# A long convolution and a bilinear layer on one core: the first layer's Strassen scheme laid over the pair of weights, in chunks of 768 tokens

## The chip, the core and the metric

The kernel runs on one core of one Trainium2 chip. A core has engines that run side by side and meet at semaphores: TensorE (PE) multiplies matrices and writes PSUM; VectorE (DVE) and ScalarE (ACT) work on SBUF and PSUM; GpSimd (POOL) works on SBUF; SyncE (SP) issues DMA transfers, which ACT's queue does too. PSUM has eight banks; one holds 512 float32 columns in each of 128 partitions. The metric is the device time of one execution in microseconds, the median of the runs.

## The reference

All is float32. For each of 8 sequences of 3072 tokens with 256 channels:

```python
X = np.fft.rfft(x, axis=1)
y = np.fft.irfft(X * (filt_r + 1j * filt_i), n=3072, axis=1)   # 256 channels
a = y @ w_a          # 256 x 1536
b = y @ w_b          # 256 x 1536
out = (a * b) @ w_out   # 1536 x 256
```

## The kernel before

Accuracy near float32 comes from splitting: each operand of a fast matmul is a rounded high part and the low rest, and a product takes three passes (high by high, high by low, low by high).

**The transforms.** A sequence is written as 128 x 24 tokens. Per sequence (a batch; the text counts them from 0 to 7) there are 12 first steps (`split_x`, `s1`, `store_z`: two rows of 24 each, through DRAM `z`), 16 second steps (`s2`: the short transform and the product with the filter on DVE; `split_y`; `is1`: the inverse short transform, into DRAM `td`), and the inverse long step `is2`, which makes the tokens of one chunk out of `tt` (loaded from `td`). The sequence has 6 chunks of 512 tokens. `is2` also makes the seven combinations of Strassen's scheme, as `ah` (high) and `al` (low): two of the four quarters come from one half of the channels, two from the other.

**The two layers.** For each chunk there are 6 visits, one for each pair `p` of 128-column blocks of the weights. In a visit each of `w_a` and `w_b` is multiplied by Strassen's scheme (the variant with seven products and shared sums): the quarters are two halves of the channels, two halves of the tokens (256 each), two blocks of the pair. A product (`product`) writes the a and the b part side by side into one bank of 512 columns, 2 x 3 matmuls of 256 columns; numbers 1, 6, 7 and 4 go to bank x, 2 to y, 5 and 3 to z. ACT copies the partial results out (lines 932, 940, 942, 968) and DVE adds the rest (937, 957, 959). `parts` multiplies a by b (line 678), `split` makes `gh` on ACT and `gl` on POOL (686, 687), and `project` adds the second layer's products into banks po0 and po1: 12 matmuls of 512 columns a visit. Every product and projection matmul is issued in `mm` (line 226), with a weight load of its own. PSUM: x has two buffers, y, z, po0, po1, f0 and f1 (transforms) one each.

**The order.** It is written out by hand. Each visit has slots 2v and 2v + 1; `plan` and `early` hold the transform steps of the next sequence and the `is2` of the next chunk. Steps of odd slots run in the next visit after product 6, steps of even slots before product 4. A visit projects one half of the visit before (`f0`) and the other half of the one before that (`f1`).

**The first sequence.** Its transforms run ahead of the first visit (the front, 91 us), with plain float32 matmuls. The weights arrive as float64 and are converted on DVE, ACT and POOL (`conv_...`: fields, power, sign, high, low, value, combine, halves); 11 of the 18 pieces before the first visit, seven beside visits (`BESIDE`, `stream_weights`). So that late weights aren't needed early, sequence 0 takes chunks 0 and 1 half by half, and `keep` holds half a sum in the buffers of the filter (line 706), which `store` adds later.

Of the kernel before, what the change touches and what calls it, by code (L numbers as in the profile page):

```python
# [19 lines left out]
N1, N2 = 128, 24  # L20
# [4 lines left out]
NC = 6  # L25
# [4 lines left out]
BESIDE = {i: (11 + i, None) for i in range(7)}  # L30
# [55 lines left out]
def _tables():  # L86
# [100 lines left out]
    gc = g.reshape(NC, 4, 128, N1).transpose(0, 2, 1, 3)  # L187
# [31 lines left out]
def fft_filter_bilinear_kernel(ctx: ExitStack, tc, x, x0, filt, fny, filt0, fny0, wa, wb, wo, s1c, gc, fc, fl, ic, sc, s1f, ff, fi, out):  # L219
# [13 lines left out]
    p2 = pool("p2", 2)  # L233
# [20 lines left out]
    ps_x, ps_h, ps_o, ps_f = pool("ps_x", 2, PSUM), pool("ps_h", 1, PSUM), pool("ps_o", 1, PSUM), pool("ps_f", 1, PSUM)  # L254
# [11 lines left out]
    def give_weights(p, where):  # L266
        wab[p] = [[where.tile([128, 7, 128], F32R, name=f"w{m}{h}{p}") for h in "hl"] for m in "ab"]
# [23 lines left out]
    def conv_fields(w):  # L291
        if streaming:
            sc = bank_f([128, 512], I32, streaming[-1])
        else:
            sc = ps_x.tile([128, 512], I32, name="sc", tag="x")
# [29 lines left out]
    spare, pair = [], {}  # L325
# [119 lines left out]

    def s2(b, i):
        zt, fr, fm = held.pop(("z", b, i)), filts[i % 2][:, 0], filts[i % 2][:, 1]
        ps = bank_f([128, 2, D])
        turn(i, fct, flt, zt[0], zt[1], ps)
        y = later[0].tile([128, 2, D], F32, name="y", tag="e1")  # L450
# [9 lines left out]
        nc.vector.tensor_tensor(out=y, in0=y, in1=v, op=ALU.add)  # L460
# [18 lines left out]
    def first_const(n0, n1):  # L479
        if "sf" not in held:  # L480
            held["sf"] = p2.tile([128, 13, 128], F32, name="sf", tag="ah")
            held["sh"] = p2.tile([128, NI, 128], F32R, name="sh", tag="ah"), p2.tile([128, NI, 128], F32R, name="sl", tag="al")
        nc.sync.dma_start(out=held["sf"][:, n0:n1], in_=s1f[:, n0:n1])

    def first_split(i0, i1):
        (sh, sl), sf = held["sh"], held["sf"][:, i0 + 1:i1 + 1]
        nc.scalar.copy(out=sh[:, i0:i1], in_=sf)
        nc.vector.tensor_tensor(out=sl[:, i0:i1], in0=sf, in1=f32(sh[:, i0:i1]), op=ALU.subtract)
# [71 lines left out]
    def first_swap(i):  # L560
# [3 lines left out]
        if not swapped:  # L564
            swapped["w"] = p2.tile([128, 3, 2, D], F32, name="fs", tag="al")
# [38 lines left out]
    def first_t():  # L604
        tt = p2.tile([128, 4, D], F32, name="tt", tag="tt", bufs=1)
        gt = p2.tile([128, 4, N1], F32, name="gt", tag="gt", bufs=1)
        nc.sync.dma_start(out=gt, in_=gc[0])
        ah = p2.tile([128, 7, 256], F32R, name="ah", tag="ah")
        al = p2.tile([128, 7, 256], F32R, name="al", tag="al")
        held["t", 0, 0] = tt, gt, ah, al  # L610

    def load_td(tt, b, c, i, queues):

        for j, queue in enumerate(queues):
            to = tt[8 * i.start:8 * i.stop].rearrange("(p j) n d -> j p n d", j=2)[j]
            queue.dma_start(out=to, in_=td[b][i, :, 4 * c:4 * c + 4, j].rearrange("i q n d -> (i q) n d"))
# [405 lines left out]
```

## Time and profile before

| | us |
|---|---|
| median of 3 runs | 2464.78 (2461.64 to 2466.12) |
| the profiled execution | 2464.96 |
| its span, first to last instruction | 2463.2 |
| first visit starts | 91.07 |
| second sequence's visits start | 411.53 |
| sequence 3's visits start and end | 1001.85, 1297.02 |
| last sequence's visits start | 2182.52 |

The page of the profile gives each engine's busy time, the chain of work that ended last, groups of instructions with mean lengths and the idle time before them, and DMA issues. The starts of visits were read from the timeline of PE. A matmul's row is longer than the time until the next one starts, because matmuls overlap; what one costs is the distance between two starts.

### The profile page before, as it was taken

To read this page: it belongs to the slowest core of one execution; us is meant where nothing else is said; L and a number is where in the kernel's file an instruction comes from. 1 tells how busy PE (TensorE), PEld (TensorE's weight loads), DVE (VectorE), ACT (ScalarE), POOL (GpSimd) and SP (SyncE) were. 2 spreads that over 40 slices of the span, in tenths; PEclk is the share of its full clock that TensorE was granted. 3 is DMA by queue.
4 is the path that set the end of the run, shared out by engine and by line. 5 is a ranking of instruction groups with operands and counts; after the bars stand their busy time and mean duration, and the time that the engine had idled before them with its cause. 6 is when DMAs were issued, how large, how long until landed. Compare 5 with 4: busy or idle time off the path is not lost.

```text
span 2463.2 us, 46508 instructions
## 1 busy us (share of the span) xinstructions
PE 2420.0 (98%) x17478; PEld 2263.9 (92%) x17478; DVE 1780.7 (72%) x2511; ACT 1405.0 (57%) x2480; POOL 1223.0 (50%) x926
## 2 busy tenths in 40 slices
PE   7889999999999999999999999999999999999999
PEld 3588999999999999999999999999999999999998
DVE  6775996569955798568976589656996569955554
ACT  5755555555556555565555555565555655555454
POOL 4765454545545554454545545454454545534333
PEclk9999999999999999999999999999999999999999
DMA  9437442544334443245523454145432444310100
GB/s 303 160 127 239 148 134 71 171 143 142 116 102 142 152 154 114 88 146 160 159 80 112 157 158 139 63 145 166 142 121 78 161 144 149 108 39 22 44 22 18
DMA packets 209397, 310.21 MB, mean 126 GB/s; under 512 B 19186, under 2 KB 119476, under 8 KB 209092
## 3 DMA queue, kind: packets, MB, share of 16 engines
q1 hardware_dynamic: 166580, 230.55, 30.3%
q10 hardware_dynamic: 42592, 76.70, 8.9%
q8 instruction: 137, 2.24, 0.4%
q14 instruction: 88, 0.72, 0.1%
HBM read 202.31 MB, written 108.45 MB: 126 GB/s over the span
## 4 chain that ended last, share of the span: by engine, by line
PE 93%; DMA 2%; issue 2%; ACT 1%; DVE 1%; POOL 1%; SPq 0%; ACTq 0%; POOLq 0%; DVEq 0%
PE x L226 30%; PE po L226 30%; PE z L226 15%; PE y L226 7%; PE ps L635 3%; PE ps L226 3%; PE ps L441 2%; PE ps L442 2%; DMA filt<-in_filt 1%; PE ps L556 0%; POOL xl L393 0%; PE ps L524 0%; DMA zf<-z 0%; DVE g L678 0%; DMA gt<-in_gc 0%
## 5 line engine op out<-in xcount | busy, mean ns | idle before, releaser
L687 POOL TENSOR_TENSOR gl<-g,gh 128x512 fp32r<-128x512 f32 x574 | 745.1, 1301 | 788.8 <-ACT gh L686 762.5
L678 DVE TENSOR_TENSOR g<-c 128x512 f32<-128x512 f32 x576 | 509.1, 884 | 271.1 <-ACT c L968 134.0
L968 ACT COPY c<-x 128x512 f32<-128x512 f32 x288 | 169.2, 587 | 688.0 <-PE x L226 685.1
L686 ACT CAST gh<-g 128x512 fp32r<-128x512 f32 x576 | 357.1, 620 | 52.8 <-PE po L226 26.7
L226 PE MATMUL po<-gh,woh 128*128 128x512 f32 x1152 | 369.5, 388 | 2.6 <-DVE filt L706 2.6
L226 PE MATMUL po<-gl,woh 128*128 128x512 f32 x1152 | 359.8, 380 | 0.0
L226 PE MATMUL po<-gh,wol 128*128 128x512 f32 x1152 | 359.8, 380 | 0.0
L226 PE MATMUL x<-ah,wah 128*128 128x256 f32 x1152 | 316.8, 275 | 7.0 <-ACT c L932 4.5
L226 PE MATMUL x<-al,wah 128*128 128x256 f32 x1152 | 317.1, 275 | 0.1
L226 PE MATMUL x<-ah,wal 128*128 128x256 f32 x1152 | 316.9, 275 | 0.0
L226 PE MATMUL x<-ah,wbh 128*128 128x256 f32 x1152 | 316.9, 275 | 0.0
L226 PE MATMUL x<-al,wbh 128*128 128x256 f32 x1152 | 316.9, 275 | 0.0
L226 PE MATMUL x<-ah,wbl 128*128 128x256 f32 x1152 | 316.9, 275 | 0.0
L957 DVE TENSOR_TENSOR c<-x,c 128x512 f32<-128x512 f32 x288 | 197.9, 687 | 155.3 <-PE x L226 149.9
L226 PEld LDWEIGHTS po<-gl,woh 128*128 128x128 f32 x1152 | 217.3, 189 | 32.6 <-DVE gl L687 0.4
L226 PEld LDWEIGHTS po<-gh,wol 128*128 128x128 f32 x1152 | 218.3, 190 | 29.3
L226 PEld LDWEIGHTS x<-ah,wah 128*128 128x128 f32 x1152 | 219.5, 191 | 26.0 <-ACT c L932 5.9
L226 PEld LDWEIGHTS x<-al,wah 128*128 128x128 f32 x1152 | 219.6, 191 | 15.3 <-DVE al L646 0.3
L656 POOL TENSOR_TENSOR al<-t,ah 128x512 fp32r<-128x512 f32 x96 | 146.3, 1544 | 152.3 <-ACT ah L655 152.3
L226 PEld LDWEIGHTS x<-ah,wal 128*128 128x128 f32 x1152 | 221.3, 192 | 0.0
L226 PEld LDWEIGHTS x<-ah,wbh 128*128 128x128 f32 x1152 | 221.3, 192 | 0.0
L226 PEld LDWEIGHTS x<-al,wbh 128*128 128x128 f32 x1152 | 221.3, 192 | 0.0
(145 smaller groups left out, 6067.4 us busy)
## 6 DMA issues: line engine op xcount, KB each, us to landing
z<-zh ACTq DMA_DIRECT2D x112, 256.0 KB, 2.5
filt<-in_filt SPq DMA_DIRECT2D x112, 256.0 KB, 2.6
zth<-z SPq DMA_DIRECT2D x112, 256.0 KB, 3.0
tt<-td SPq DMA_DIRECT2D x94, 256.0 KB, 3.9
out<-ot SPq DMA_DIRECT2D x47, 512.0 KB, 3.0
td<-t ACTq DMA_DIRECT2D x114, 192.0 KB, 2.1
xt<-in_x SPq DMA_DIRECT2D x84, 256.0 KB, 4.2
st<-s1d SPq DMA_DIRECT2D x84, 256.0 KB, 2.7
```

What stands on the lines that cost most here:

```text
L226: nc.tensor.matmul(out, w, m, **kw)
L441: nc.tensor.matmul(out, w[:, 0], hi, start=True, stop=False)
L442: nc.tensor.matmul(out, wl[:, 0], lo, start=False, stop=True)
L635: nc.tensor.matmul(to, tt[:, n, 128 * k:128 * k + 128], gt[:, n].rearrange("p (k a) -> p k a", k=2), start=True, stop=True)
L656: nc.gpsimd.tensor_tensor(out=al[:, 3 + i:5 + i], in0=t[:, i:i + 2], in1=f32(ah[:, 3 + i:5 + i]), op=ALU.subtract)
L678: nc.vector.tensor_tensor(out=gt, in0=g[:, :, 0], in1=g[:, :, 1], op=ALU.mult)
L686: nc.scalar.copy(out=gh, in_=gt)
L687: low.tensor_tensor(out=gl, in0=gt, in1=f32(gh), op=ALU.subtract)
L957: nc.vector.tensor_tensor(out=c1[:, 1], in0=bx, in1=c1[:, 1], op=ALU.add)
L968: nc.scalar.copy(out=c1[:, 0], in_=bx)
```

## The change

Strassen's scheme is laid over the pair (w_a, w_b): its two column blocks are now the same 128 columns of `w_a` and of `w_b`, where they were two blocks of one matrix. One unit `u` of 12 is a visit; a product has three matmuls, and its result is one half of the tokens of a chunk. A chunk has 768 tokens, so there are 4 a sequence, 48 visits a sequence for 36, and a product's matmul has 384 columns. The projection of a visit has 768 columns: 512 in po0 or po1 and 256 in po2, which both output halves share. x and y have one bank each and swap roles from visit to visit.

Moved: the add of `y` and `v` to POOL (`add_y`), and the filter's DVE work to the end of the visit (`late`); low halves of `al` from POOL to DVE; the stores of z from ACT's queue to SP's; part of the output copies from DVE to ACT; both halves of a visit are projected two visits later; `ah` and `al` lie in alternating pools. The slots of the transform steps are new: second steps stand four slots apart in most sequences, `is2` comes in four pieces, and first steps begin before the end of the round before. Sequence 0 takes its chunks in plain order, and `keep` is gone.

```diff
-NC = 6
+NC = 4
+NM = N2 // NC
+TH = NM // 2 * N1
+FULL = 512
-BESIDE = {i: (11 + i, None) for i in range(7)}
+BESIDE = {v: (11 + i, None) for i, v in enumerate((0, 1, 2, 4, 5, 6, 7))}
...
-    ps_x, ps_h, ps_o, ps_f = pool("ps_x", 2, PSUM), pool("ps_h", 1, PSUM), pool("ps_o", 1, PSUM), pool("ps_f", 1, PSUM)
+    ps_h, ps_o, ps_f = pool("ps_h", 1, PSUM), pool("ps_o", 1, PSUM), pool("ps_f", 1, PSUM)
...
     def conv_value(w):
-        v = f32(t) if k == 2 else pair[p][:, k, 0:4].rearrange("p a n -> p (a n)")
-        nc.gpsimd.tensor_tensor(out=v, in0=f32(t), in1=f32(s), op=ALU.mult)
+        if k == 2:
+            nc.gpsimd.tensor_tensor(out=t, in0=t, in1=s, op=ALU.mult)
+        else:
+            for i in range(2):
+                nc.gpsimd.tensor_tensor(
...
     def store_z(b, i):
-        nc.scalar.dma_start(out=zd[b][0][:, 2 * i:2 * i + 2], in_=f32(zh))
+        nc.sync.dma_start(out=zd[b][0][:, 2 * i:2 * i + 2], in_=f32(zh))
...
-        nc.vector.tensor_tensor(out=y, in0=y, in1=v, op=ALU.add)
+    def add_y(b, i):
+        y, v = held["y", b, i]
+        nc.gpsimd.tensor_tensor(out=y, in0=y, in1=v, op=ALU.add)
...
     def is2(b, c, k):
+        if k > 1:
+            i = 2 * k - 4
             nc.scalar.copy(out=ah[:, 3 + i:5 + i], in_=t[:, i:i + 2])
-            nc.gpsimd.tensor_tensor(out=al[:, 3 + i:5 + i], in0=t[:, i:i + 2], in1=f32(ah[:, 3 + i:5 + i]), op=ALU.subtract)
+            v.tensor_tensor(out=al[:, 3 + i:5 + i], in0=t[:, i:i + 2], in1=f32(ah[:, 3 + i:5 + i]), op=ALU.subtract)
+            return
...
-    def product(b, c, p, i, bank, first=False):
+    def product(b, c, u, i, bank, first=False):
         m, n = FACTORS[i]
-        for k in range(2):
-            wh, wl = wab[p][k]
-            for q, (w, v) in enumerate(((wh, ah), (wh, al), (wl, ah))):
-                mm(
-                    bank[:, k], w[:, m], v[:, n], start=first and k == 0 and q == 0, stop=q == 2, skip_group_check=True
-                )
+        ah, al = held["t", b, c][2:]
+        wh, wl = wab[u // 2][u % 2]
+        for q, (w, v) in enumerate(((wh, ah), (wh, al), (wl, ah))):
+            mm(bank, w[:, m], v[:, n], start=first and q == 0, stop=q == 2, skip_group_check=True)
...
+    def project(r, i):
+        passes = [(k, q, *w) for q, w in enumerate(((wo_h, gh), (wo_l, gh), (wo_h, gl))) for k in range(2)]
+        if begins or ends:
+            passes.sort(key=lambda e: e[0] if begins else -e[0])
+        for k, q, w, g in passes:
+            to, g = (po[2][:, i], g[:, FULL:]) if k else (po[i], g[:, :FULL])
...
+    def store(r, i):
+        if i:
+            nc.vector.tensor_copy(out=ot[:, :, FULL:], in_=po[2])
+        nc.scalar.copy(out=ot[:, i, :FULL], in_=po[i])
...
+                bx, bz = bank("xy"[v % 2]), bank("z")
+                product(b, c, u, 1, bx, True)
+                nc.scalar.copy(out=c00, in_=bx)
+                if prev:
+                    split(prev[-1], 0)
+                product(b, c, u, 5, bz, True)
+                nc.scalar.copy(out=c10, in_=bz)
+                by = bank("yx"[v % 2])
+                product(b, c, u, 2, by, True)
+                convert(1)
+                product(b, c, u, 6, bx)
+                nc.scalar.copy(out=c01, in_=bx)
+                if prev:
+                    split(prev[-1], 1)
+                convert(3)
+                for what, at_slot in after:
+                    run(what, at_slot)
+                run(early, slot)
+                if one:
+                    project(one, 0)
...
+                product(b, c, u, 7, bx)
+                nc.vector.tensor_tensor(out=c10, in0=bx, in1=c10, op=ALU.add)
+                nc.vector.tensor_tensor(out=c00, in0=by, in1=c00, op=ALU.add)
+                product(b, c, u, 3, bz)
+                nc.vector.tensor_tensor(out=c01, in0=bz, in1=c01, op=ALU.add)
+                nc.vector.tensor_tensor(out=c01, in0=c01, in1=c10, op=ALU.mult)
+                convert(5)
+                run(plan, slot)
+                if one:
+                    project(one, 1)
...
+                product(b, c, u, 4, bx)
+                nc.scalar.copy(out=c11, in_=bx)
+                nc.vector.tensor_tensor(out=c00, in0=c00, in1=c11, op=ALU.mult)
+                r["gated"] = c01, c00
+                for fn, *args in late:
+                    fn(*args)
```

## Rows read from the trace of the kernel before

**Rows 1.** The page, parts 1 (busy time by engine) and 4 (chain that ended last)

```profile
PE 2420.0 (98%) x17478; PEld 2263.9 (92%) x17478; DVE 1780.7 (72%) x2511; ACT 1405.0 (57%) x2480; POOL 1223.0 (50%) x926
...
PE 93%; DMA 2%; issue 2%; ACT 1%; DVE 1%; POOL 1%; SPq 0%; ACTq 0%; POOLq 0%; DVEq 0%
```

**Rows 2.** Windows: length, each engine's busy us (instructions), PE clock, DMA; three stretches

```profile
91.07:411.53 320.46, 301.98 (x2165) 282.48 (x2166) 249.11 (x351) 187.68 (x333) 178.56 (x130) 0.99 0.45 145
91.07:165.10 74.03, 62.73 (x430) 56.69 (x431) 62.90 (x94) 47.99 (x83) 54.56 (x36) 0.98 0.29 102
1001.85:1297.02 295.17, 295.17 (x2185) 281.14 (x2183) 219.52 (x305) 170.50 (x302) 148.25 (x113) 1.00 0.42 131
```

**Rows 3.** Timeline of PE, one visit of batch 7: start us, us, instruction

```profile
2182.52 0.28 PE L226 MATMUL x<-ah,wah 128*128 128x256 f32 x1
...
2186.49 0.27 PE L226 MATMUL x<-ah,wah 128*128 128x256 f32 x1
...
2187.83 0.60 PE L226 MATMUL po<-gh,woh 128*128 128x512 f32 x2
...
2189.80 0.28 PE L226 MATMUL x<-ah,wah 128*128 128x256 f32 x1
```

**Rows 4.** The page, part 5: weight loads (PEld) | busy, mean ns | idle before

```profile
L226 PEld LDWEIGHTS po<-gh,wol 128*128 128x128 f32 x1152 | 218.3, 190 | 29.3
...
L226 PEld LDWEIGHTS x<-ah,wal 128*128 128x128 f32 x1152 | 221.3, 192 | 0.0
```

**Rows 5.** Groups of instructions by shape, batch 3: ACT, DVE, POOL

```profile
L686 ACT CAST gh<-g 128x512 fp32r<-128x512 f32 x72 | 44.7, 621 | 5.8 <-DVE g L678 3.3 <-PE po L226 2.4
...
L968 ACT COPY c<-x 128x512 f32<-128x512 f32 x36 | 21.1, 587 | 87.6 <-PE x L226 87.6
...
L957 DVE TENSOR_TENSOR c<-x,c 128x512 f32<-128x512 f32 x36 | 24.7, 687 | 16.5 <-PE x L226 15.8
...
L687 POOL TENSOR_TENSOR gl<-g,gh 128x512 fp32r<-128x512 f32 x72 | 93.6, 1303 | 93.8 <-ACT gh L686 92.5 <-PE x L226 1.3
```

**Rows 6.** Groups by shape, ACT, the last 23 us

```profile
L725 ACT COPY ol<-po 128x256 f32<-128x256 f32 x1 | 0.4, 372 | 2.3 <-PE po L226 2.3
```

**Rows 7.** Timeline of all engines from 95.6 to 96.9 us

```profile
95.67 0.49 DVE L299 TENSOR_SCALAR t<-raw 128x512 int32<-128x512 int32 x1
...
95.83 0.28 PE L226 MATMUL x<-ah,wbl 128*128 128x256 f32 x1
96.14 0.58 ACT L942 COPY c<-x 128x512 f32<-128x512 f32 x1
...
96.78 0.19 PEld L226 LDWEIGHTS x<-ah,wah 128*128 128x128 f32 x1 [0.86 <-ACT c L942]
```

**Rows 8.** Waits of PE in batch 0: us in total, times, longest us

```profile
PE x L226 <- ACT c L932: 4.5, 6, 1.4
...
PE po L226 <- DVE filt L706: 2.6, 2, 1.9
```

**Rows 9.** Groups by shape, POOL and DVE, 91 to 165 us

```profile
L687 POOL TENSOR_TENSOR gl<-g,gh 128x512 fp32r<-128x512 f32 x14 | 19.0, 1354 | 13.7 <-ACT gh L686 13.7
...
L656 POOL TENSOR_TENSOR al<-t,ah 128x512 fp32r<-128x512 f32 x4 | 5.5, 1388 | 2.6 <-ACT ah L655 2.6
...
L299 DVE TENSOR_SCALAR t<-raw 128x512 int32<-128x512 int32 x7 | 8.9, 1269 | 0.0
...
L339 DVE TENSOR_TENSOR m<-m 128x256 f32<-128x256 f32 x12 | 4.5, 419 | 0.1
```

**Rows 10.** Timeline of all engines from 78 to 99 us

```profile
77.83 2.11 POOL L339 TENSOR_TENSOR m<-m 128x256 f32<-128x256 f32 x3
...
88.83 2.02 PE L635 MATMUL ps<-gt,tt 128*128 128x128 f32 x16 [1.86 <-DMA tt<-td]
```

**Rows 11.** Timeline of all engines from 2450 us on

```profile
2452.56 0.69 DVE L678 TENSOR_TENSOR g<-c 128x512 f32<-128x512 f32 x1
```

**Rows 12.** The page, part 6: DMA issues, KB each, median us to landing

```profile
tt<-td SPq DMA_DIRECT2D x94, 256.0 KB, 3.9
```

More of the change, by code (lines that the diff above doesn't have):

```diff
@@ L266, in give_weights @@
     def give_weights(p, where):
-        wab[p] = [[where.tile([128, 7, 128], F32R, name=f"w{m}{h}{p}") for h in "hl"] for m in "ab"]
+        wab[p] = [[where.tile([128, 7, 128], F32R, name=f"w{m}{h}{p}") for h in "hl"] for m in "ef"]
     for p in range(NP - LATE):
@@ new lines, in is2 @@
+            held["t", b, c] += [where.tile([128, 7, TH], F32R, name=n, tag=n, bufs=1) for n in ("ah", "al")]
+            ah, al = held["t", b, c][2:]
+            t = held["b", b, c] = moe[0].tile([128, 4, TH], F32, name="t", tag="ot")
+            ps = is2_half(b, c, 0, 0)
+            nc.scalar.copy(out=t[:, 1], in_=ps)
+            ps = is2_half(b, c, 0, 1)
+            nc.scalar.copy(out=ah[:, 0], in_=t[:, 1])
+            v.tensor_tensor(out=t[:, 0], in0=ps, in1=t[:, 1], op=ALU.subtract)
@@ new lines, in product, with piece, split @@
+        wh, wl = wab[u // 2][u % 2]
+        for q, (w, v) in enumerate(((wh, ah), (wh, al), (wl, ah))):
+            mm(bank, w[:, m], v[:, n], start=first and q == 0, stop=q == 2, skip_group_check=True)
+    def bank(name):
+        return ps_h.tile([128, TH], F32, name=name, tag=name)
+    def piece(name, bufs=1):
+        return moe[0].tile([128, TH], F32, name=name, tag=name, bufs=bufs)
+    def split(r, h, low=nc.gpsimd):
+        if "g" not in r:
+            r["g"] = [moe[0].tile([128, 2, TH], F32R, name=n, tag=n, bufs=2) for n in ("gh", "gl")]
+        (gh, gl), gt = r["g"], r["gated"][h]
+        nc.scalar.copy(out=gh[:, h], in_=gt)
+        low.tensor_tensor(out=gl[:, h], in0=gt, in1=f32(gh[:, h]), op=ALU.subtract)
@@ L856, in fft_filter_bilinear_kernel @@
         steps(POST)
-        is2(0, 0, 0)
-        is2(0, 0, 1)
+        for k in range(4):
+            is2(0, 0, k)
         steps(LAST)
@@ new lines, in fft_filter_bilinear_kernel, with at, run @@
+        FORMED = (
[3 rows of a table added]
+        )
+        ROUND = 2 * NC * NF
+        plan, early = {}, {}
+        def at(slot, fn, *args, when=plan):
+            when.setdefault(slot, []).append((fn, *args))
+        def run(what, slot):
+            for fn, *args in what.pop(slot, ()):
+                fn(*args)
+        at(7, nc.sync.dma_start, s1d, s1c)
+        for t, v, d in ((fct, fc, fcd), (flt, fl, fld), (ict, ic, icd)):
+            at(8, nc.sync.dma_start, d, v)
+            at(10, nc.sync.dma_start, f32(t), d)
@@ L919, in run @@
-            def run(what, slot):
-                for fn, *args in what.get(slot, ()):
-                    fn(*args)
-            for v, (c, p) in enumerate(VISITS if b == 0 else [(c, p) for c in range(NC) for p in range(NP)]):
-                slot = 2 * v
-                halves = b == 0 and c < 2
-                convert = (lambda site: stream_weights(v, site)) if b == 0 else (lambda site: None)
-                r = {"at": (b, c, p), "from": NP // 2 if halves and p >= NP // 2 else 0, "to": NP // 2 - 1 if halves and p < NP // 2 else NP - 1}
-                bx, by, bz = bank("x"), bank("y"), bank("z")
-                c0 = moe[0].tile([128, 2, 2, 256], F32, name="c0", tag="c0")
-                c1 = r["c1"] = moe[0].tile([128, 2, 2, 256], F32, name="c1", tag="c1", bufs=2)
-                product(b, c, p, 1, bx, True)
-                nc.scalar.copy(out=c0[:, 0], in_=bx)
-                product(b, c, p, 2, by, True)
-                if prev:
-                    split(prev[-1], "f0")
-                    parts(prev[-1], prev[-1]["c1"], "f1")
-                nc.vector.tensor_tensor(out=c0[:, 0], in0=by, in1=c0[:, 0], op=ALU.add)
+                        at(t, load_z, n, i + 3)
```

305 lines of the change are left out of this document (136 added, 169 removed), and 3 rows, old and new, of the table FORMED.

## The prediction

> **What bounds the kernel now.** I read the page first: TensorE (PE) is busy 98% of the span and the chain that ended last is 93% PE [rows 1]. Busy time alone proves little, since matmuls are pipelined, so I cut the span into batches. Batch 3 shows PE busy for 295.17 of 295.17 us while VectorE (DVE) has 219.5, ScalarE (ACT) 170.5 and GpSimd (POOL) 148.3 us of work [rows 2]; the view of waits names none of PE's between 411 and 2453 us. So from batch 1 on the time is what PE needs to issue its matmuls. Batch 0 takes 320.46 us [rows 2], 25.3 more, in waits. The front takes 91 us. The profiled execution took 2464.96 us, 1.76 more than its span and 0.2 from the median of the runs; I sum against it.
>
> What a matmul costs is read from start to start, not from its row's length. In a visit without transform steps, twelve matmuls of 256 columns start between 2186.49 and 2187.83 us: 111.7 ns each. The whole visit, 42 of these and 12 of 512 columns, takes 7.28 us, so one of 512 takes (7280 - 42 x 111.7) / 12 = 215.8 ns [rows 3]. These are not in proportion: 0.4215 ns a column at 512, 0.436 at 256. The weight loads say why: in a stream of 256 the loader has no idle time ahead of its loads, beside 512 it has 29.3 us over 1152 [rows 4]. So a matmul of 256 waits a little for its weights; one of 384 should not.
>
> **The change, part by part.**
>
> *Products.* Each product now runs for one unit (128 columns of each first-layer matrix) over half a chunk of 768 tokens. Before: 288 visits x 42 = 12096 matmuls of 256 columns, 1351.1 us. After: 384 visits x 21 = 8064 of 384, the same number of columns. No row shows 384, so I bound it: at the rate of 512 it is 161.9 ns; on the line through 256 and 512 it is (111.7 + 215.8) / 2 = 163.75. I take 512 less 128 columns at 2.4 GHz, the level granted in this stretch (1.00 [rows 2]): 215.8 - 53.3 = 162.4, since 384 lies with 512 on the side where the loader has time. 8064 x 162.4 = 1309.6 us: -41.5 (bounds -45.6 and -30.6).
>
> The Trainium skill, page "TensorE: Matmul & The Clock Gate", section "Back-to-back issue gap", gives a spacing of N/2.4 + 2.5 ns, so 109.2 for 256: there the trace differs with its 111.7, and for 512 it agrees (215.8). By the page alone only 2880 fixed costs of 2.5 ns would go, an estimate of 7 us.
>
> *Projections.* 3456 matmuls of 512 (745.8 us) become 2304 of 512 and 2304 of 256, for 768 columns are split 512 and 256: 2304 x (215.8 + 111.7) = 754.6 us, +8.8. A plain visit is then 21 x 162.4 + 6 x 327.5 ns = 5.375 us. The transforms and the inverse step keep their matmuls.
>
> *PE's waits inside a visit.* PSUM has one x, y and z bank in turn, where x had two. The evacuations shrink with the tile: an ACT copy from PSUM takes 587 ns for 512 [rows 5] and 372 for 256 [rows 6], hence 480 for 384; a DVE add 687 and 419 [rows 5, 9], hence 553; a POOL subtraction 1303 and 703 [rows 5, 10], hence 1.0 us. How soon an evacuation starts and ends a wait: the last matmul into x starts at 95.83 us and its copy at 96.14, 0.2 us after the matmul's slot; the copy ends at 96.72 and the next weight load starts at 96.78 [rows 7]. So a product wants its bank free one load (112 ns) and 60 ns ahead of its start. Count from the end of the last product (number 4) of the visit before, 0.487 us a product: numbers 1, 5, 2 and 6 start at 0, 0.487, 0.974 and 1.461. Number 4's copy runs from 0.20 to 0.68; number 2, in that bank, wants it by 0.80. Number 1's copy runs from 0.69 to 1.17; number 6 wants it by 1.29. Both have 0.12 us to spare. Behind them ACT has a cast (621 ns for 512 [rows 5], 513 by the same slope), number 5's copy and, from 2.15 to 2.63, number 6's copy; number 7, behind a projection of 0.98 us, wants it by 2.76. DVE's adds have 0.5 us each. So I cost these waits at nothing, with up to 10 us in the range. What keeps this cover is ACT's written order: its transform steps come after number 6's copy, and numbers 7 and 3 and a projection stand before number 4's.
>
> *Moved steps.* The add of y and v goes from DVE to POOL and its filter products to the visit's end; low halves of `al` go from POOL to DVE; output copies of 512 go to ACT; stores of z go from ACT's queue to SP's. There they wait for `zl`, and the loads of x and `tt` that are issued behind them wait too; those are issued two or three visits (11 to 17 us) ahead and land in 3.9 us [rows 12]. By the durations above ACT gains some 17 us a batch, to 188 of 291; DVE and POOL stay near 220 and 155. None becomes the bound: 0.
>
> *Batch 0.* Its 25.3 us of waits fall in two stretches. Visits 0 to 7 take 74.03 us [rows 2] against 8 x 7.28 and two inverse steps of 16 matmuls (2.02 us with the last one's whole length [rows 10], some 1.8 in a stream), 61.8: 12.2 lost. PE's waits there name ACT copies and kept sums [rows 8], but POOL is busy for 54.56 of 74.03 us [rows 2], and DVE's instructions with both ends in SBUF are stretched: `t` takes 1269 ns in the mean [rows 9] and 0.49 us at 95.67 [rows 7]. At their short lengths, 15 `g` of 0.69 [rows 11], 7 `t` of 0.49, 12 `m` and two `al` of 0.42 are 19.7 us; with POOL's 54.56 that is 74.3 of 74.03: they took turns. The Trainium skill's page "SBUF — State Buffer", section "Who interferes with whom", says that VectorE with two SBUF inputs and a reading GpSimd block each other; the trace agrees with that sum.
>
> After, the same conversion lies beside visits 0 to 9 (53.7 us of PE). POOL: the 54.56 less 19.0 of `gl` and 5.5 of `al` [rows 9], plus 18 `gl` of 1.0 and 0.8 for six products cut in halves: 48.9. DVE in SBUF: 20 gatings of 0.55, `t` and `m` as before, two `al` of 768 columns (0.95): 21.9. Together 70.8: 17.1 lost, +5. The second stretch loses 13.1 now (25.3 - 12.2), with two first-transform steps a visit; after, there are four in three visits, and the copies of kept sums (2.6 us of wait [rows 8]) are gone: I take half, -7. Batch 0: -2, bounds -15 and +14.
>
> *Ends.* At the start `tt` and the first inverse step carry 6 rows, not 4: +1.5 (0 to +4). At the end stands the same chain of copy, gating, split, projection, copy and store, with larger stores: +0.5 (-1.5 to +1.5).
>
> Sum: -41.5 + 8.8 - 2 + 1.5 + 0.5 = -32.7 on 2464.96: 2432 us. Its own range, the ends not being met all at once, is 2415 to 2452.
>
> **The rivals.**
> 1. *Slower: ACT is late at the x bank.* A copy that starts more than 0.12 us late stops PE. If one transform cast of 621 ns stands before it, the visit loses 0.5 us; PE's 32.7 us are gone after 66 such visits of 384. Were it so in the 28 visits a batch that hold a transform step, 196 in all, it would cost 98 us: 2530. For it: ACT works in order, and only ACT frees these banks. Against it: the written order above. 0.13, of which 0.05 that it eats about the gain and 0.08 that it costs more.
> 2. *The 5 ns above 106.7 belong to every matmul short of 512.* Then 384 takes 165.0, and the products win 20.5, not 41.5: 2453. For it: no row shows 384. Against it: the loader's idle time [rows 4]. 0.08.
> 3. *The first ten visits stay locked and run into the first transform:* the two stretches lose 25 and 13: 2447. For it: the turn-taking above fills its stretch whole. Against it: POOL's subtractions have a whole visit of slack now. 0.06.
>
> **How the numbers follow.** The forecast, 2432, has 0.73. Runs of this kernel tell 0.2% (5 us) from no change. Faster: 0.73 + 0.08 + 0.06 = 0.87; within 0.2%: 0.05; slower: 0.08. The range is the forecast's, stretched over rivals 2 and 3 to 2458; above it lies rival 1.
>
> **What would show it.** Matmuls of 384 start 162.4 ns apart; a visit without transforms takes 5.37 to 5.38 us in batch 7; batches 1 to 6 take 291.1 us each, PE busy throughout; batch 0 takes 314. Visits of 5.8 us in which PE waits for ACT's copies of products 1 or 4 would be rival 1; 165 ns rival 2; batch 0 above 325 us rival 3. A steady batch longer than 295 us would prove the forecast wrong.

## The result and the profile after

| | before | after |
|---|---|---|
| median of the runs, us | 2465.45 (2461.64 to 2467.92) | 2436.00 (2434.91 to 2436.50) |
| the profiled execution | 2464.96 | 2434.91 |
| its span | 2463.2 | 2433.0 |

The changed kernel takes 0.9881 of the time before [0.9864, 0.9898], 29 us less. The forecast was 2432: right, 4 us too low. The page of the changed kernel, in the parts that answer to [rows 1] and [rows 12] (busy time; the chain that ended last; two groups with count, busy time and mean length; one DMA issue with its time to landing):

```profile
PE 2389.0 (98%) x14598; PEld 2264.0 (93%) x14598; DVE 1587.5 (65%) x2811; ACT 1447.0 (59%) x3103; POOL 1241.9 (51%) x1146
...
PE 91%; DVE 2%; DMA 2%; POOL 2%; issue 1%; ACT 1%; SPq 0%; ACTq 0%; POOLq 0%; DVEq 0%
...
L997 ACT COPY c<-x 128x384 f32<-128x384 f32 x192 | 92.0, 479 | 424.5 <-PE x L229 421.4
...
L985 DVE TENSOR_TENSOR c<-x,c 128x384 f32<-128x384 f32 x192 | 107.0, 558 | 291.8 <-PE x L229 159.9
...
tt<-td SPq DMA_DIRECT2D x62, 384.0 KB, 5.2
```

TensorE still ends last, with 2880 fewer matmuls. The evacuations have the lengths that were interpolated: 479 ns for an ACT copy of 384 columns (480 forecast), 558 for a DVE add (553). Now the windows of the changed kernel, to be laid beside [rows 2]: the front, batch 0, batch 3, the last batch to the end of the span, the first ten visits, and the part of them at half the clock (length; busy time of PE, weight loads, DVE, ACT, POOL with their instructions; PE clock, DMA share, GB/s).

```profile
0.00:92.96 92.96, 72.30 (x188) 32.83 (x189) 65.08 (x105) 54.73 (x92) 49.24 (x50) 1.00 0.90 286
92.96:413.99 321.03, 302.00 (x1825) 283.68 (x1824) 237.41 (x388) 200.05 (x418) 189.88 (x166) 0.98 0.49 154
997.44:1288.67 291.23, 291.23 (x1824) 281.31 (x1823) 190.11 (x342) 175.27 (x380) 152.07 (x140) 1.00 0.42 132
2158.13:2433.00 274.87, 270.52 (x1681) 262.02 (x1680) 144.93 (x277) 145.39 (x322) 96.76 (x96) 1.00 0.08 28
...
92.96:165.54 72.58, 59.46 (x321) 53.26 (x320) 63.44 (x97) 48.08 (x93) 49.36 (x41) 0.93 0.30 101
95.46:105.70 10.24, 8.65 (x26) 7.60 (x26) 6.92 (x14) 5.13 (x10) 0.00 (x0) 0.50 0.01 2
```

In batch 3 PE is busy for the whole 291.23 us, and 291.1 was forecast. The timeline of PE in the last batch shows what a plain visit is made of (start us, us, instruction; x2 is one matmul of 512 and one of 256):

```profile
2179.64 0.33 PE L229 MATMUL x<-ah,weh 128*128 128x384 f32 x1
2179.80 0.33 PE L229 MATMUL x<-al,weh 128*128 128x384 f32 x1
...
2181.59 0.49 PE L229 MATMUL po<-gh,woh 128*128 128x512 f32 x2
2181.91 0.49 PE L229 MATMUL po<-gh,wol 128*128 128x512 f32 x2
2182.24 0.49 PE L229 MATMUL po<-gl,woh 128*128 128x512 f32 x2
2182.57 0.33 PE L229 MATMUL x<-ah,weh 128*128 128x384 f32 x1
...
2185.02 0.33 PE L229 MATMUL y<-ah,wfh 128*128 128x384 f32 x1
```

The visit lasts from 2179.64 to 2185.02, 5.38 us. Its twelve matmuls of 384 ahead of the projection take 2181.59 - 2179.64 = 1.95 us, 162.5 ns each, and three pairs take 0.98 us, 327 a pair.

Stretch by stretch the span compares so (batches by the start of their first product):

| stretch | before | after | difference | forecast |
|---|---|---|---|---|
| front | 91.07 | 92.96 | +1.9 | +1.5 |
| batch 0 | 320.46 | 321.03 | +0.6 | -6.1 |
| batches 1 to 6 | 1770.99 | 1744.14 | -26.9 | -24.5 |
| last batch and end | 280.68 | 274.87 | -5.8 | -3.6 |
| span | 2463.2 | 2433.0 | -30.2 | -32.7 |

One part of this is only a shift: four first steps of the sequence after the next, 0.67 us each, now run in batch 0 already; two more move into batch 1, and batch 6 is shorter for having six fewer (287.21 us). In batch 0 that is 2.7 us. Without it batch 0 is 318.3, which is 318.3 - 291.1 = 27.2 us over a steady batch, against 25.3 before and 23.3 forecast. This is the one term that went the other way.

PE loses more than these figures say, before and after, for the first visits have nothing to project yet: batch 0 has 276 pairs, not 288 (before, 414 matmuls of 512, not 432), 3.9 us less work than a steady batch both times. So the losses are 31.1 us after and 29.2 before. In the first ten visits PE's own work is 210 matmuls of 384, 48 pairs and 12 matmuls of the inverse step (0.112 us each: a visit of the last batch that holds twelve takes 6.72 us, not 5.38), together 51.2 us. These visits take 72.58 us, so they lose 21.4, and the rest of batch 0 loses 9.7.

PE's waits in batch 0 of the changed kernel (what PE stood before, what it waited for: us in total, times, longest), to be read beside [rows 8]:

```profile
PE x L229 <- ACT c L964: 4.1, 3, 1.7
PE ps L229 <- POOL xl L405: 4.0, 5, 1.2
PE y L229 <- ACT c L964: 3.4, 3, 1.4
PE y L229 <- DVE c L985: 2.3, 3, 1.0
```

With the smaller ones, PE's named waits in the first ten visits are 13.1 us of the 21.4. Matmuls at half the clock (below) are some 4 more. The remaining 4 are in the main what twelve waits cost beyond their idle time: the row of the matmul before a wait runs on for 0.17 us past its slot, and the first matmul after it takes 0.27 us to the next, not 0.16. Line 964 is ACT's copy of product 1. Why it is late is seen in the timeline of the third visit (start, length, instruction, idle time before it and its releaser):

```profile
110.41 1.36 DVE L989 TENSOR_TENSOR c<-c,c 128x384 f32<-128x384 f32 x1
...
111.69 0.68 DVE L315 SCALAR_TENSOR_TENSOR s<-raw,ps 128x512 int32<-128x512 int32 x1
111.70 2.10 POOL L363 TENSOR_TENSOR wel<-m,weh 128x896 fp32r<-128x896 f32 x1 [0.35 <-ACT weh L362]
112.29 1.92 DVE L998 TENSOR_TENSOR c<-c,c 128x384 f32<-128x384 f32 x1
112.40 0.60 ACT L322 ACTIVATE ps<-t 128x512 f32<-128x512 int32 x1
112.94 0.47 ACT L964 COPY c<-x 128x384 f32<-128x384 f32 x1
113.46 0.19 PEld L229 LDWEIGHTS x<-ah,weh 128*128 128x128 f32 x1 [2.00 <-ACT c L964]
```

ACT's step of the weight conversion, `high` (line 322), stands ahead of the copy in ACT's order and waits for DVE's `sign` (315); DVE came late to it because an earlier multiplication (line 989) took 1.36 us, not 0.56; and the next one (998) takes 1.92 us, beside POOL's subtraction of 896 columns.

### The profile page after: what moved, and what is told of

It is laid out like the page before. It is cut to its first block, busy times and chain, and to the rows that moved or that the text cites. A ratio compares the mean times of both kernels' runs of the same rounds, so it can differ in the third digit from the quotient of the medians.

```text
span 2433.0 us, 41173 instructions
## 1 busy us (share of the span) xinstructions
PE 2389.0 (98%) x14598; PEld 2264.0 (93%) x14598; DVE 1587.5 (65%) x2811; ACT 1447.0 (59%) x3103; POOL 1241.9 (51%) x1146
## 4 chain that ended last, share of the span: by engine, by line
PE 91%; DVE 2%; DMA 2%; POOL 2%; issue 1%; ACT 1%; SPq 0%; ACTq 0%; POOLq 0%; DVEq 0%
PE po L229 30%; PE x L229 19%; PE y L229 19%; PE z L229 15%; PE ps L659 3%; PE ps L229 2%; PE ps L454 2%; PE ps L453 2%; DMA filt<-in_filt 1%; POOL gl L717 1%; POOL xl L405 0%; DVE c L989 0%; DMA gt<-in_gc 0%; DVE c L985 0%; PE ps L551 0%
## 5 line engine op out<-in xcount | busy, mean ns | idle before, releaser
L717 POOL TENSOR_TENSOR gl<-c,gh 128x384 fp32r<-128x384 f32 x766 | 774.9, 1012 | 1123.3 <-ACT gh L716 1108.3
L229 PE MATMUL po<-gh,woh 128*128 128x512 f32 (+1 forms) x1536 | 401.8, 330 | 0.0
L716 ACT CAST gh<-c 128x384 fp32r<-128x384 f32 x768 | 396.1, 516 | 3.4 <-DVE c L998 2.7
L229 PE MATMUL po<-gl,woh 128*128 128x512 f32 (+1 forms) x1536 | 398.0, 327 | 0.1
L229 PE MATMUL po<-gh,wol 128*128 128x512 f32 (+1 forms) x1536 | 397.8, 327 | 0.0
L998 DVE TENSOR_TENSOR c<-c,c 128x384 f32<-128x384 f32 x384 | 221.5, 577 | 142.1 <-ACT c L997 141.8
L229 PEld LDWEIGHTS po<-gh,woh 128*128 128x128 f32 x1536 | 271.6, 190 | 14.8
L229 PE MATMUL x<-ah,weh 128*128 128x384 f32 x768 | 253.1, 330 | 5.6 <-ACT c L964 4.1
L229 PE MATMUL y<-ah,wfh 128*128 128x384 f32 x768 | 252.4, 329 | 6.2 <-ACT c L964 3.4
L229 PE MATMUL x<-al,weh 128*128 128x384 f32 x768 | 251.0, 327 | 0.0
L989 DVE TENSOR_TENSOR c<-c,c 128x384 f32<-128x384 f32 x384 | 228.7, 596 | 13.1
L988 DVE TENSOR_TENSOR c<-z,c 128x384 f32<-128x384 f32 x384 | 210.5, 548 | 0.0
```

The costliest lines, as they stand in the source:

```text
L229: nc.tensor.matmul(out, w, m, **kw)
L716: nc.scalar.copy(out=gh[:, h], in_=gt)
L717: low.tensor_tensor(out=gl[:, h], in0=gt, in1=f32(gh[:, h]), op=ALU.subtract)
L988: nc.vector.tensor_tensor(out=c01, in0=bz, in1=c01, op=ALU.add)
L989: nc.vector.tensor_tensor(out=c01, in0=c01, in1=c10, op=ALU.mult)
L998: nc.vector.tensor_tensor(out=c00, in0=c00, in1=c11, op=ALU.mult)
```

## The experiments

After the result two theories stood for the waits of the first ten visits. *Turn-taking*, as in the prediction: DVE's instructions with both ends in SBUF and POOL's shut each other out, so the stretch is as long as the sum of both. *The DVE queue*, the rival: PE waits for what DVE hands over in order, through ACT; POOL counts only by what it stretches on DVE. For the rest, each step of the prediction is tried by itself. All edits are made to the changed kernel, and changes of time are against its 2436.0 us.

### What a matmul costs by its width: e1_streams

```diff
+STREAMS = (
+    ((512, 128),), ((256, 128),), ((384, 128),), ((320, 128),), ((256, 96),), ((384, 96),), ((256, 64),),
+    ((512, 128), (256, 128)), ((448, 128),), ((256, 128),),
+)
...
+        for i in range(COUNT):
+            columns, rows = forms[i % len(forms)]
+            mm(bank[0:rows, 0:columns], w[:, 128 * (i % 4):128 * (i % 4) + rows], m[:, 0:columns])
```

> This kernel leaves the whole computation out: it issues ten streams of 48 matmuls each, every one with its own weight load and with nothing to wait for. In order: 512 columns, 256, 384, 320 with 128 weight columns; 256 and 384 with 96; 256 with 64; 512 and 256 by turns; 448; 256 again. Theory (256 waits for the load of 128 weight columns, 384 does not): 215.8 ns for 512, 162.5 for 384, 135.8 for 320, 189 for 448, 111.7 for 256 with 128 weight columns but 109.2 with 96 and with 64; 327.5 for a pair of 512 and 256. Rival (each matmul short of 512 bears about 5 ns of its own): 165 for 384, 138 for 320, and 111.7 for 256 whatever the weights' columns.

COUNT is 48, and `rows` are the weight columns. Start to start, in ns: 512 columns 215.8, 448 189.2, 384 162.5, 320 135.8, 256 111.7, all with 128 weight columns. From 320 to 512 the slope is 80 / 192 = 0.417 ns a column, and on that line 256 would take 109.1. That is what it takes with 96 or 64 weight columns: 109.1 both times. With 96, 384 stays at 162.5. So 2.6 ns of 256's time are the wait for 128 weight columns, 384 has none of it, and rival 2 (165 ns) falls. 512 and 256 in turn take 327.5 a pair, the sum that the projections were costed with. Start to start the pair divides as 218 from the 512 to the 256 and 109 from there on, here and in the changed kernel alike: the 2.6 ns of the 256 are paid in full, ahead of it. If the loads of a pair could share their time, it would take 215.8 + 109.1 = 324.9.

The Trainium skill, page "TensorE: Matmul & The Clock Gate", section "Back-to-back issue gap", has N/2.4 + 2.5 ns as the gap of a matmul by itself; every width here agrees within 0.2 ns except 256 with a full load. For streams in which each matmul has its load the same section gives a shorter spacing at 512, about 131 ns; the 215.8 here do not bear that out.

### Rival 1's price: e2_cast_first

```diff
-                nc.scalar.copy(out=c00, in_=bx)
                 if prev:
                     split(prev[-1], 0)
+                nc.scalar.copy(out=c00, in_=bx)
```

> One thing changed in the kernel after: the 384-column cast of the visit before stands ahead of the copy of product 1 on ScalarE. Theory (that copy has 0.12 us to spare before product 6): it starts at about 1.0 us instead of 0.69 after the last product of the visit before, ends at 1.48 where 1.29 is wanted, and each of the 384 visits loses 0.2 us: 75 us, 2510. A plain visit of the last sequence takes 5.58 us for 5.38. Rival (the copy is covered by more than I count): 2436, visits of 5.38 us.

2507.47 us in a single run, +71.5. A plain visit takes 5.54 us for 5.38, and batch 3 8.3 us more. The timeline of a plain visit of this kernel (start, length, instruction; its line 966 is 964 of the changed kernel), and below it the same copy in the changed kernel's visit that starts at 2179.64:

```profile
2244.97 0.33 PE L229 MATMUL x<-ah,weh 128*128 128x384 f32 x1
...
2245.54 0.51 ACT L716 CAST gh<-c 128x384 fp32r<-128x384 f32 x1
2245.95 0.48 ACT L966 COPY c<-x 128x384 f32<-128x384 f32 x1
2246.49 0.19 PEld L229 LDWEIGHTS x<-ah,weh 128*128 128x128 f32 x1 [0.19 <-ACT c L966]
2246.49 0.43 PE L229 MATMUL x<-ah,weh 128*128 128x384 f32 x1
```

```profile
2180.38 0.48 ACT L964 COPY c<-x 128x384 f32<-128x384 f32 x1
```

Product 1's copy ends at 2246.43, 1.46 us into the visit, and the load for product 6 starts 0.06 us later, as in [rows 7]. The prediction wanted the bank free by 1.29: 0.17 late, and the visit is 0.16 longer. In the changed kernel the same copy ends at 2180.86, 1.22 us into its visit, so the cover is real but is 0.07 us, not 0.12.

### The first ten visits: e3_low_dve, e4_combine_pool, e12_no_low

```diff
 # e3_low_dve: low halves of streamed weights on DVE, not POOL
-            nc.gpsimd.tensor_tensor(out=wl, in0=v, in1=f32(wh), op=ALU.subtract)
+            (nc.vector if streaming else nc.gpsimd).tensor_tensor(out=wl, in0=v, in1=f32(wh), op=ALU.subtract)
 # e4_combine_pool: sums of weight blocks on POOL, not DVE
-                (nc.vector if streaming else nc.gpsimd).tensor_tensor(out=m[:, :, o], in0=m[:, :, a], in1=m[:, :, b], op=op)
+                nc.gpsimd.tensor_tensor(out=m[:, :, o], in0=m[:, :, a], in1=m[:, :, b], op=op)
 # e12_no_low: streamed low halves not worked out; a DMA fills their place
-            nc.gpsimd.tensor_tensor(out=wl, in0=v, in1=f32(wh), op=ALU.subtract)
+            if streaming:
+                nc.sync.dma_start(out=f32(wl), in_=v)
+            else:
+                nc.gpsimd.tensor_tensor(out=wl, in0=v, in1=f32(wh), op=ALU.subtract)
```

> One thing changed in the kernel after: beside the visits of the first sequence, the low halves of the converted weights are made on VectorE, not on GpSimd. Theory (in visits 0 to 9 VectorE's work inside SBUF and GpSimd's take turns): 17.7 us of GpSimd work (six of 896 columns at 2.1, four of 512 at 1.28) become 9.2 of VectorE's, the turn-taking shrinks from 70.7 to 62 us, the first sequence's visits from 321 to some 313 us: 2428. Rival (VectorE's own queue bounds these visits): it gets 9 us more, 330 us and 2445.

> One thing changed in the kernel after: beside the visits, the twelve additions of 256 columns that combine the converted weights are made on GpSimd, not on VectorE. Theory (turn-taking): 12 x (0.70 - 0.42) = 3.4 us more, 2439. Rival (VectorE's queue): 5 us less there, 2431.

> A part of the computation is left out of the kernel after: beside the visits of the first sequence the low halves of the converted weights are not subtracted on GpSimd; a transfer from SyncE's queue puts the unrounded values in their place, so GpSimd loses some 17.7 us of work and no engine gains any. Theory 1 (work inside SBUF of VectorE and GpSimd takes turns): 70.7 less 17.7 leaves less than TensorE's 53.7 us; visits 0 to 9 take 58 to 62 us for 72.6, about 2424. Theory 2 (VectorE's queue): its instructions are stretched less, by 3 to 6 us; 66 to 70 us, 2430 to 2433. Theory 3 (neither sum; the order in which the queues wait for each other): 71 to 73 us, 2434 to 2437.

The window of the first ten visits, first of e3_low_dve, then of e4_combine_pool, then of e12_no_low (columns as above; the changed kernel has 72.58, with DVE 63.44 and POOL 49.36):

```profile
93.23:171.38 78.15, 62.00 (x320) 55.86 (x320) 64.38 (x106) 47.70 (x93) 31.68 (x29) 0.91 0.26 91
```

```profile
92.32:162.88 70.56, 58.56 (x320) 52.52 (x320) 58.89 (x85) 47.67 (x93) 58.37 (x52) 0.95 0.30 99
```

```profile
95.45:164.28 68.83, 58.12 (x322) 52.22 (x321) 54.93 (x98) 48.02 (x94) 29.48 (x31) 0.95 0.50 172
```

The times are 2440.72 (0.9900 of before [0.9885, 0.9914]), 2433.15 (0.9876 [0.9857, 0.9894]) and 2432.91 (0.9874 [0.9858, 0.9891]). Work taken from POOL and given to DVE makes the stretch 5.6 us longer; work taken from DVE and given to POOL makes it 2.0 shorter, where turn-taking wanted the reverse. The third is the clearest: 20 us of POOL's work are gone, the sum of turns would have fallen to some 58 to 62 us, and the stretch loses 3.8, inside the 66 to 70 us of that run's second theory. So the turns don't fill it.

About half of each change is idle time of PE: the length less PE's busy time is 13.1 us in the changed kernel and 16.2, 12.0 and 10.7 in the three runs. The other half is PE's own matmuls, for the clock was at 0.50 for 10.2 us of the changed kernel's stretch and for some 14, 7 and 7 of theirs (their mean clock is 0.91, 0.95 and 0.95, not 0.93). Longer waits and more time at half the clock go together here, and with one profiled execution each these runs don't part them; the idle time alone points the same way.

What POOL does is stretch DVE, as two groups show, first of the changed kernel in its first ten visits, then of e12_no_low, where they are lines 992 and 1001 (count | busy us, mean ns | idle before):

```profile
L998 DVE TENSOR_TENSOR c<-c,c 128x384 f32<-128x384 f32 x9 | 10.2, 1132 | 0.0
L989 DVE TENSOR_TENSOR c<-c,c 128x384 f32<-128x384 f32 x10 | 9.5, 948 | 0.3
```

```profile
L992 DVE TENSOR_TENSOR c<-c,c 128x384 f32<-128x384 f32 x10 | 6.2, 621 | 0.3
L1001 DVE TENSOR_TENSOR c<-c,c 128x384 f32<-128x384 f32 x9 | 5.7, 637 | 0.3 <-ACT c L1000 0.3
```

The multiplications go from 0.95 and 1.13 us to 0.62 and 0.64. The timeline of the changed kernel shows how exact this is. Of its 768 multiplications 626 do not start while POOL works, and none of these takes more than 0.56 us. Forty take longer than 0.65 us; all forty started beside a POOL instruction, and 39 of them end 0.41 or 0.42 us after it does, as both in the timeline of the third visit do (the second at 114.21, POOL's subtraction at 113.80). DVE's adds of product results, which read one operand from PSUM, take at most 0.58 us in all 947 cases that start beside POOL. The Trainium skill, page "SBUF — State Buffer", section "Who interferes with whom", states that a VectorE instruction with two SBUF inputs contends with a GpSimd instruction that reads SBUF; the trace agrees. That the stretch is the sum of both engines' work does not follow, and is not so.

### Is DVE's time alone the bound? e9_gate_pool, e5_high_later, e11_best

```diff
 # e9_gate_pool: first multiplication of visits 0 to 9 on POOL
-                nc.vector.tensor_tensor(out=c01, in0=c01, in1=c10, op=ALU.mult)
+                (nc.gpsimd if b == 0 and v < 10 else nc.vector).tensor_tensor(out=c01, in0=c01, in1=c10, op=ALU.mult)
 # e5_high_later: ACT's high after product 6's copy, what follows it later; pieces in visits 0 to 6 (in part)
...
-            5: ((0, conv_sign), (1, conv_combine)), 6: ((0, conv_high),),
+            3: ((1, conv_high), (3, conv_halves), (0, conv_power), (2, conv_value)),
+            5: ((0, conv_sign), (1, conv_low), (2, conv_combine)),
...
 # e11_best: e4_combine_pool, e9_gate_pool and e6_fill (below) in one
```

> One thing changed in the kernel after: in visits 0 to 9 of the first sequence the first of the two multiplications of a by b is made on GpSimd, not on VectorE. Theory (VectorE's queue, in its order, bounds these visits): it loses ten instructions of 0.55 us bare and 0.95 as they stand there; visits 0 to 9 take 67 to 69 us for 72.6, 2431 to 2433. Rival (VectorE's work inside SBUF and GpSimd's take turns): 10 x (1.0 - 0.55) = 4.5 us more, 2440.

> One thing changed in the kernel after: beside the visits of the first sequence, ScalarE's step 'high' of the weight conversion comes after the copy of product 6 of the next visit, not at the end of its visit ahead of the next copy of product 1; 'low' and the steps behind it move one visit later, and the pieces start in visits 0 to 6. Theory (ScalarE stands in 'high', waiting for VectorE's 'sign' for 5.3 us in all, and the copy of product 1 queued behind it stops TensorE for 7.5 us): these waits go, the first sequence's visits take 314 to 316 us for 321, 2430. Rival (VectorE's queue as a whole bounds these visits): 321 us, 2436, the waits only change their names.

> Three edits at once in the kernel after: the combining additions on GpSimd (e4), the first multiplications of visits 0 to 9 on GpSimd (e9), the 14 matmuls that fill the first visit's wait (e6). Theory (VectorE's queue): e4's 3 us and e9's add up, and with VectorE relieved the fill is worth some of its 4 us: 2427 to 2430. Rival (GpSimd, with some 68 us of work, becomes the bound of visits 0 to 9): 2433 to 2440.

The first ten visits of e9_gate_pool, and ACT's wait in them:

```profile
95.83:177.63 81.80, 63.91 (x320) 56.30 (x320) 57.86 (x87) 47.87 (x94) 58.71 (x51) 0.89 0.25 84
```

```profile
ACT gh L716 <- POOL c L989: 7.6, 4, 3.1
```

2446.02 us (0.9919 [0.9901, 0.9937]). DVE has 5.6 us less to do than in the changed kernel and the stretch is 9.2 longer (4.8 of it idle time of PE; the clock's mean is 0.89), so the DVE queue as a mere sum falls too. The multiplication now stands behind POOL's subtractions of 2.1 us, ACT's cast waits for it, and behind the cast in ACT's order stand the copies that free the banks. e11_best does the same with still less on DVE (46.47 us) and more on POOL (66.96): 82.53 us for the stretch, 2447.64 in all (0.9925 [0.9908, 0.9942]).

e5_high_later gains nothing: 2435.52 (0.9878 [0.9863, 0.9893]), first ten visits 73.33. PE's wait for product 1's copy falls from 7.5 to 1.3 us, but DVE's add of line 985 then costs it 4.6 at the y bank, where it cost 1.0, and ACT's copy of line 997 another 2.1. Most of the wait changes its name. The third visit itself, from 112.58 us, has no named wait left, yet takes 7.55 us for 7.58: just before it PE had stood 2.4 us for that add, and the clock was at 0.50 from 112.7 to 116.1.

What fits all of these runs is a ring of engines that work in order and hand over to one another: DVE (`sign`, adds, multiplications, stretched by POOL) to ACT (`high`, casts, copies) to PE and back. It gains from work taken off DVE as long as nothing for which ACT waits is put behind POOL's long instructions. This is argued from the runs, not shown by one of its own: which hand-over carries how much of the 21.4 us, and how much of them is the clock, stays open.

### The half clock: e6_fill

```diff
+            if (b, c, u, i, q) == (0, 0, 0, 5, 1):
+                fill(6)
...
+    def fill(n):
+        ps = ps_o.tile([128, FULL], F32, name="ps", tag="po1")
+        for _ in range(n):
+            mm(ps, wo_h[0][:, 0, 0:128], wo_h[0].rearrange("p f d -> p (f d)"), start=True, stop=True)
...
+                if v == 0 and b == 0:
+                    fill(8)
```

> One thing changed in the kernel after: in the first visit, while TensorE waits for the inputs of product 5, it issues 14 matmuls of 512 columns whose result nobody reads (8 ahead of product 5, 6 behind its first matmul). Theory (the granted clock of 0.50 between 97 and 105.4 us follows on that wait, and costs 25 matmuls 157 ns each): the clock stays at full speed, the first sequence's visits take 317 us for 321, 2432. Rival (the clock falls anyway, or the added matmuls delay the product): 2436 to 2438.

These are 14 matmuls of 512 columns in the first visit, ahead of product 5's first and second pass, that nobody reads. In the changed kernel TensorE was granted 0.50, the 1.2 GHz level, from 95.46 to 105.70 us (window above); the fall came just after a wait of 1.5 us for the first `ah`, and a wait of 1.0 for the first `al` lies inside. 26 matmuls were issued in that time, 320 ns apart where nothing held them, not 162.5: some 4 us. Two windows of e6_fill, its first and its sixth visit:

```profile
98.01:106.17 8.16, 7.36 (x38) 6.09 (x37) 6.01 (x11) 4.72 (x8) 0.00 (x0) 0.98 0.01 2
134.62:144.26 9.64, 7.63 (x35) 6.68 (x35) 8.92 (x12) 5.58 (x11) 7.79 (x6) 0.82 0.56 167
```

With the filling the clock is 0.98 in the first visit, which takes 8.16 us, not 10.45. But the second takes 8.08 for 6.67, with PE waiting longer for DVE and ACT: of the 4 us, 0.9 are left. After five visits the kernel with the filling is 1.65 us ahead. In the sixth the clock falls to 0.50 for 3.4 us, after a wait of 1.5 us for product 1's copy (the changed kernel waits 1.4 there and keeps its clock), and that visit takes 9.64 us, not 7.24. So the ten visits take 72.51 us for 72.58, and the kernel 2434.35 (0.9878 [0.9862, 0.9893]). The forecast gain did not come: part of the slow matmuls' 4 us lay beside other waits, and the half clock came back elsewhere. What it costs by itself this run can't say.

### The moved steps: e7_add_dve, e8_al_pool, e10_z_act

```diff
 # e7_add_dve
-        nc.gpsimd.tensor_tensor(out=y, in0=y, in1=v, op=ALU.add)
+        nc.vector.tensor_tensor(out=y, in0=y, in1=v, op=ALU.add)
 # e8_al_pool: al of the last four of the seven combinations back on POOL
-            v.tensor_tensor(out=al[:, 3 + i:5 + i], in0=t[:, i:i + 2], in1=f32(ah[:, 3 + i:5 + i]), op=ALU.subtract)
+            nc.gpsimd.tensor_tensor(out=al[:, 3 + i:5 + i], in0=t[:, i:i + 2], in1=f32(ah[:, 3 + i:5 + i]), op=ALU.subtract)
 # e10_z_act: all stores of z back on ACT's queue; one of three lines
-        nc.sync.dma_start(out=zd[b][0][:, 2 * i:2 * i + 2], in_=f32(zh))
+        nc.scalar.dma_start(out=zd[b][0][:, 2 * i:2 * i + 2], in_=f32(zh))
```

> One move undone in the kernel after: the add of y and v is on VectorE again, behind the filter products. Theory (VectorE's adds of product results have 0.5 us to spare, no engine is the bound, the move to GpSimd is worth nothing): 2436, steady batches of 291.1 us. Rival (the add, 0.7 us or, where it meets GpSimd, 1.3, makes the add of product 7 late for product 4): up to 0.2 us in each of 112 visits, 2440 to 2458.

> One move undone in the kernel after: the low halves of the last four combinations of the inverse step (768 columns at a time) are on GpSimd again. Theory (they are ready a visit ahead of their first product either way): 2436. Rival (GpSimd needs some 1.9 us for 768 columns by the slope of its subtractions, and a new chunk's first visit waits): 31 chunks by up to 1 us, 2440 to 2467.

> One move undone in the kernel after: the stores of z are issued from ScalarE's queue again. Theory (they stand behind product 6's copy, with 2.4 us until the next copy that TensorE needs): 2436, steady batches of 291.1 us. Rival (their issue, 0.33 to 0.39 us each, and their wait for the low half make the copies of products 4 and 1 late): up to 0.2 us in each of 84 visits, 2440 to 2453.

The add back on DVE: 2451.53 us (0.9941 [0.9926, 0.9956]), +15.5, and batch 3 takes 293.36. DVE has 210.5 us of work there, far from full. The timeline of the visit that loses most:

```profile
1063.05 0.75 DVE L470 SCALAR_TENSOR_TENSOR y<-ps,sct,filt 128x512 f32<-128x512 f32 x1
1063.82 1.51 DVE L472 SCALAR_TENSOR_TENSOR v<-ps,sct,filt 64x512 f32<-64x512 f32 x2
1065.37 0.42 DVE L477 TENSOR_TENSOR y<-ps,nyq 1x256 f32<-1x256 f32 x1
1065.83 0.71 DVE L484 TENSOR_TENSOR y<-y,v 128x512 f32<-128x512 f32 x1
1066.57 0.56 DVE L985 TENSOR_TENSOR c<-y,c 128x384 f32<-128x384 f32 x1
...
1067.18 0.43 PE L229 MATMUL y<-ah,wfh 128*128 128x384 f32 x1 [0.27 <-DVE c L985]
```

The filter's work and the add are one run of 3.5 us on DVE, the add that frees a bank (line 985) stands behind it and ends at 1067.13, and this visit takes 5.91 us where it had 5.38. It alone holds the multiplication of line 477, which comes once a batch; the others that are hit lose 0.04 to 0.18 us (5.85 for 5.82, 5.91 for 5.81), some 22 of 48, and the batch 2.1. The rival of this run is borne out.

`al` back on POOL: 2449.67 us (0.9933 [0.9917, 0.9950]), +13.7, batch 3 293.26. One of its visits takes 6.54 us, not 5.82, one loses 0.17 and four 0.28 or 0.29. The timeline of the first:

```profile
1065.56 1.82 POOL L684 TENSOR_TENSOR al<-t,ah 128x768 fp32r<-128x768 f32 x1
1065.71 2.08 DVE L989 TENSOR_TENSOR c<-c,c 128x384 f32<-128x384 f32 x1
...
1067.84 0.51 ACT L716 CAST gh<-c 128x384 fp32r<-128x384 f32 x1 [1.01 <-DVE c L989]
1068.25 0.47 ACT L968 COPY c<-z 128x384 f32<-128x384 f32 x1
1068.62 0.48 ACT L973 COPY c<-x 128x384 f32<-128x384 f32 x1
...
1069.16 0.43 PE L229 MATMUL x<-ah,weh 128*128 128x384 f32 x1 [0.46 <-ACT c L973]
```

This is the ring again, in one visit of a steady batch: POOL's subtraction stretches a multiplication from 0.56 to 2.08 us, ACT's cast waits for it, the copies behind the cast start late, and PE stands. That is not the rival's path (a new chunk that waits for its `al`), but its price.

The stores of z back on ACT's queue: 2439.23 (0.9894 [0.9876, 0.9912]), batch 3 291.04 where the changed kernel has 291.23. This move is worth nothing that these runs can tell.

No kernel tried is clearly faster than the changed one: the lowest medians with the whole computation, 2433.15 and 2434.35, are within the spread of their runs (2432.16 to 2440.66). The start of the first visit alone lies between 92.3 and 98.0 us in the profiles of these kernels.

## Why the prediction was right, and where it was off

- *Products and projections* (-41.5 and +8.8): right. 162.5 ns a matmul of 384, 327.5 a pair, 5.38 us a plain visit, 291.03 to 291.23 us for batches 2 to 5. The choice of 512's side rather than the line through 256 and 512, made from the loader's idle time [rows 4], is what e1_streams bears out.
- *PE's waits inside a visit* (nothing): right. Between 414 and 2424 us the view of waits names none; what is left to spare is 0.07 us at number 6. The way of counting was right to 0.02 us (e2_cast_first), the cover 0.05 smaller than counted. Rival 1 did not occur, and its price per visit hangs on how late the copy is: 0.16 us for one cast ahead of it, not the 0.5 of a whole one, for the cast begins 0.57 us into the visit, before the copy could.
- *Moved steps* (nothing): right for the change as it stands, but the reason was too weak. It went by sums over a batch, by which no engine becomes the bound. By sums e7_add_dve and e8_al_pool would cost nothing either, and they cost 15.5 and 13.7 us. What decides is which long instruction stands directly ahead of an evacuation, or stretches one that does. DVE's sum was also off: 190.1 us in batch 3, not near 220; with the add of y and v back on it (e7_add_dve) it is 210.5, 18.1 of the difference the 16 adds. ACT has 175.3, not 188.
- *Batch 0* (-2): wrong in sign, the term that was mis-sized; it measured +2, from 25.3 to 27.2 us over a steady batch. The sum of turns gave 70.8 us for the first ten visits, and they took 72.58, but that sum is refuted by e3, e4 and e12, so its nearness is luck. PE's own work beside it was counted wrong: 61.8 and 53.7 us have every visit project and, before, two inverse steps. The visits hold 336 matmuls of 256, 78 of 512 and 16 of the inverse step before (56.2 us), and 51.2 us after. So the first stretch lost 17.9 us and loses 21.4, +3.5 where +5 was forecast. What failed is the -7 for the second stretch, half of its loss, taken off without a sum: it lost 11.3 and loses 9.7, -1.6. The waits for kept sums are gone, but PE waits there 4.0 us for POOL's low halves of x (line 405), for which it waited 2.1 before.
- *Ends* (+1.5 and +0.5): +1.9, and -0.9 at the end (8.9 us from the start of the last product's last matmul, 9.8 before). The front varies by 5.7 us between the profiles of kernels that share it, so +1.9 is no measurement of the change.
- The measured sum: batches 2 to 5 last 291.13 us in the mean, so products and projections bring 8 x (291.13 - 295.17) = -32.3; with +2 for batch 0, +1.9 and -0.9 that is -29.3. The span is 30.2 us shorter; the other 0.9 lie in the last batch.
- What was said to show it: 162.4 ns, the plain visit and the steady batches are there; batch 0 is 321 (318.3 without the steps that moved into it), not 314, short of the 325 that would have been rival 3.

## What to carry to other kernels

Cost a matmul from start to start, and ask whether its weight load fits beside it: 256 columns just don't hide 128 weight columns, 320 do, and from there on columns are all that is paid. Where banks are reused within one visit, go through the written order of the engine that frees them and count the spare time of each evacuation. Sums of busy time over a batch say nothing on it; an add of 1.1 us in the mean (line 484 on DVE), 16 times a batch in the wrong place, cost 15 us here with the engine 72% busy.

## What was not expected of the hardware

- A multiplication with both ends in SBUF that takes 0.56 us alone took 2.08 beside a POOL subtraction of 1.82: it ended 0.41 us after POOL's. So do 39 of the 40 long ones of the changed kernel, to 0.01 us: DVE waits for POOL's instruction to end. Yet over ten visits the time isn't the sum of both engines' work.
- Ten microseconds at half the clock (0.50 granted, 320 ns a matmul) could be filled away where they were, and the ten visits became 0.07 us shorter: other waits took up most of the 4 us, and the clock fell again in the sixth visit.
- A 256 among 512s still pays for its weight load: 327.5 ns for the pair is 215.8 + 111.7. Start to start it comes as 218 and 109, so the spacing of one matmul in a mixed stream is not its price.
